# Folding mirrored places before the 49-point products of a Fourier mixer

## Chip, cores and metric

The kernel runs on one core of a Trainium2 chip. The metric is device time in microseconds (us) of one execution. Before the change, three runs took 1089.32, 1090.04 and 1090.96 us, a median of 1090.04 us.

## What is computed

Three layers follow each other on tensors of 2 batches x 3136 tokens x 256 features: a gated attention, a mixer with low rank along the tokens and a two-layer perceptron, and a Fourier mixer with the same kind of perceptron behind it. The change touches the Fourier mixer alone. Cut to what matters:

```python
scores = matmul(z, z.T) / S
x = u * matmul(maximum(scores, 0) ** 2, v)        # attention
u1 = x + ((x.T @ U) @ V).T
x = u1 + maximum(u1 @ w_ch1, 0) @ w_ch2           # first perceptron
X = fft(fft(x, axis=1), axis=2)                   # 3136 tokens, 256 features
u2 = x + real(X)
un = (u2 - mean(u2)) / sqrt(var(u2) + 1e-6)
return u2 + maximum(un @ w2_ch1, 0) @ w2_ch2      # second perceptron
```

## The kernel before

The 3136 tokens are ordered as 64 x 49, so the transform along the tokens is one of length 49 and then one of length 64, and the one along the features is made last. The program has an attention part (up to about 503 us) and a perceptron part. The second goes through 28 chunks of 448 tokens (layer, batch, seventh), and each chunk through 8 steps. One step is written to TensorE in a fixed order: six products of `hidden` (L431 to L433) and six of `project` (L456 to L458) for the hidden part of two steps ago, each 128x128 by 448 columns in float32r with the operands split into a high and a low half. Behind these twelve come the step's guests: the events of the 49-point transform, and one piece of each active generator (`prep1` with the product L321, `fourier` with the products L1179 and L1197 to L1202, `prep2` for the norms). Every engine works its own instructions in the order written; nothing is reordered by a scheduler there. The tables at the end of the program (`starts`, `events`, `folds`, `behind`) set the step of each guest.

The 49-point transform of a batch is made in 8 blocks of 4 token columns (`halves49`). For each block four events follow one another:

- `fold(i)` adds mirrored features on VectorE into `y`, turns them, and writes them to DRAM (`nat_d`).
- `fetch(i)` loads them back with places on partitions (98 rows by 4x128 columns).
- `tokens(i)` makes the high half on ScalarE and the low half on VectorE, and an alternating sum on VectorE.
- `axis49(i)` calls `dft49`: three float32r products of 512 columns (L1140 to L1142) into one PSUM tile, one copy on ScalarE (L133, tile `wst`), and the write to DRAM (`scr`).

Four rows of the 98 belong to each pair of mirrored places, and place 0 has two.

`fourier(b)` starts with `column128`, which treats feature 128 apart: a row is loaded into `raw128`, transposed on TensorE (L1151), split, and multiplied by the same 49-point matrix with 64 columns. Then come the 64-point products (`axis64`, L1179, plain float32, fetched from `scr`) and the feature products (`features`).

All these products take their PSUM tile from `misc()`, which hands out the banks m, x and g in turn. A product that gets a bank waits until the readers of its last content are done:

```python
def misc():
    p, tag = misc_pools[misc_at[0] % len(misc_pools)]
    misc_at[0] += 1
    return p.tile([128, 512], F32, tag=tag, name="ps_" + tag)
```

A plain float32 product stands in the trace as two MATMUL records, each with its own weight load.

Of the kernel before, what the change touches and what calls it, by code (L numbers as in the profile page):

```python
# [24 lines left out]
KPOS = 25  # L25
# [61 lines left out]
def _constants():  # L87

    o1, o2, c1, c2, tok, feat = _orders()
    b49 = np.zeros((98, 128))  # L90
    t2 = 2 * np.pi * ((c2 * np.outer(o2, np.arange(KPOS))) % 49) / 49
    for par in range(2):
        b49[par::2, par * 32 : par * 32 + KPOS] = np.cos(t2)
        b49[par::2, 64 + par * 32 + 1 : 64 + par * 32 + KPOS] = np.sin(t2[:, 1:])
# [28 lines left out]
def program(ctx, tc, zT, v, uT, U, V, w1a, w2a, w1b, w2b, b49, f64, fd, rep, mask, out):  # L123
# [52 lines left out]
    b49h = const.tile([128, 128], F32R, name="b49h")  # L176
    b49l = const.tile([128, 128], F32R, name="b49l")
# [848 lines left out]
    raw128 = mp.tile([128, 112], F32, tag="raw128", name="raw128", bufs=1)  # L1026
# [5 lines left out]
    top = [mp.tile([98, 32], F32, tag=f"top{b}", name=f"top{b}", bufs=1) for b in range(NB)]  # L1032
# [8 lines left out]
    nats = [[mp.tile([128, 512], F32R, tag=f"{t}{k}", name=f"{t}{k}", bufs=1) for t in ("nh", "nl")] for k in range(3)]  # L1041

    def pair_late():
# [6 lines left out]
    def mixer():  # L1050
# [18 lines left out]
        for x in (*nats[0], *nats[1], *nats[2]):  # L1069
            nc.gpsimd.memset(f(x)[96:128], 0.0)  # L1070
# [8 lines left out]
    def halves49(b):  # L1079
# [3 lines left out]
        yv = y[:, 0:392].rearrange("p (s m r) -> p s m r", m=49, r=2)  # L1083

        def fold(i):

            s0, s1 = 4 * i, 4 * i + 4
            for t0, t1 in ((0, 1), (1, s1)) if s0 == 0 else ((s0, s1),):
                for m, w in ((0, 0), (1, 25), (25, 1)):
                    n = 24 if m else 1  # L1090
                    in1 = x1[:, t0:t1, w : w + n]
                    if t0:
                        in1 = in1[:, :, :, ::-1]
                    tt(
                        out=yv[:, t0 - s0 : t1 - s0, m : m + n],
# [3 lines left out]
                    )  # L1099
            yt = mp.tile([128, 416], F32, tag="A1" if i == 7 else "yt", name="yt", bufs=1)  # L1100
# [6 lines left out]
            if i == 7:  # L1107
                load(out=raw128[0:32, 0:98], in_=xT[b][0:1, 1, :].rearrange("o (s p) -> o s p", p=98))

        def alternating(i, x):  # L1110

            v = x[0:98].rearrange("p (s d r) -> p s d r", s=4, r=2)
            t = spare[0:98, 0:256].rearrange("p (s d) -> p s d", s=4)
            sub(t, v[:, :, :, 0], v[:, :, :, 1])
            nc.vector.reduce_sum(out=top[b][0:98, 4 * i : 4 * i + 4], in_=t, axis=mybir.AxisListType.X)

        def fetch(i):
            h, l = nat[i] = pair_late()
            load(
                out=f(l)[0:98].rearrange("p (s d) -> p s d", s=4),  # L1120
                in_=nat_d[b][i, 0:392].rearrange("(s p) d -> p s d", p=98),
            )

        def tokens(i):
            h, l = nat[i]
            hcopy(h[0:98], f(l)[0:98])
            alternating(i, f(l))
            sub(l[0:98], f(l)[0:98], f(h[0:98]))

        def axis49(i):  # L1130
            ps = misc()
            dft49(ps, *nat.pop(i))
            w = mp.tile([128, 512], F32, tag="wst", name="wst")
            hcopy(w, ps)
# [4 lines left out]
    def dft49(ps, h, l):  # L1139
        mm(ps, b49h, h, start=True, stop=False)  # L1140
        mm(ps, b49h, l, start=False, stop=False)
        mm(ps, b49l, h, start=False, stop=True)  # L1142

    def fourier(b):
# [3 lines left out]
        def column128():  # L1148

            ps = misc()  # L1150
            nc.tensor.transpose(ps[0:98, 0:128], raw128[:, 0:98], ident)  # L1151
            h, l = (t[:, 0:64] for t in pair_late())
            for s, x in ((slice(0, 32), ps[0:98, 0:32]), (slice(32, 64), top[b][0:98])):
                hcopy(h[0:98, s], x)
                sub(l[0:98, s], x, f(h[0:98, s]))
            yield
            yield
            ps = misc()
# [260 lines left out]
```

## Time and profile before

| | before |
|---|---|
| median of three runs | 1090.04 us |
| profiled execution, its own time | 1089.02 us |
| span of the profile | 1087.2 us |
| PE busy | 1077.7 us (99%) |
| DVE busy | 848.1 us (78%) |
| ACT busy | 623.2 us (57%) |
| POOL busy | 255.2 us (23%) |
| granted TensorE clock | 1.0 |

The span runs from the first to the last instruction; 1.8 us of the execution's own time lie around it. PE is TensorE's products, PEld its weight loads, DVE is VectorE, ACT ScalarE, POOL GpSimd, SP SyncE. A MATMUL's recorded length is its passage through the array and not the time it takes from its successors; what it costs is the distance from its start to the start of the next.

### The profile page before, as it was taken

Reading aid. Unit: us, or ns where it says so; the run is one execution under the profiler, and the core shown is the slowest. Engines: PE = TensorE matmul, PEld = TensorE weight load, DVE = VectorE, ACT = ScalarE, POOL = GpSimd, SP = SyncE. Lnnn points to the kernel's source line nnn. Section 1 sums busy time; section 2 is a strip of 40 time slices with the busy share of each in tenths; the row PEclk is TensorE's granted clock in tenths of the full one; section 3 lists DMA queues with packets and bytes.
Section 4 is the critical chain, followed back from the end, with each engine's and each line's share of the span. In section 5 each row is a group of like instructions: output and inputs, shape, how many; then the busy total and the mean of one; then the engine's idle time right before and its main releaser. Section 6 shows DMA issues by size and latency. Waiting matters only on the chain.

```text
span 1087.2 us, 21197 instructions
## 1 busy us (share of the span) xinstructions
PE 1077.7 (99%) x7926; PEld 1000.6 (92%) x7926; DVE 848.1 (78%) x1571; ACT 623.2 (57%) x1094; POOL 255.2 (23%) x426
## 2 busy tenths in 40 slices
PE   9999999999999999999999999999999999999998
PEld 7999999999989999989899999999999999999997
DVE  7898888988999987666666776677688888778863
ACT  7888777768897876553434444433355454444431
POOL 2143345222333344221110121121231111011100
PEclk9999999999999999999999999999999999999999
DMA  6356667675667677875523453231253221121210
GB/s 177 94 135 167 179 184 218 210 268 143 167 189 209 177 216 241 268 244 154 183 68 90 143 177 100 78 78 34 64 128 105 62 89 47 35 65 47 60 43 35
DMA packets 140519, 146.04 MB, mean 134 GB/s; under 512 B 72534, under 2 KB 113530, under 8 KB 140416
## 3 DMA queue, kind: packets, MB, share of 16 engines
q1 hardware_dynamic: 108704, 70.57, 22.9%
q0 software_dynamic: 23280, 47.72, 15.5%
q10 hardware_dynamic: 8432, 26.40, 7.7%
q8 instruction: 62, 1.02, 0.4%
q14 instruction: 41, 0.34, 0.1%
HBM read 88.61 MB, written 56.00 MB: 133 GB/s over the span
## 4 chain that ended last, share of the span: by engine, by line
PE 84%; DMA 5%; DVE 4%; ACT 3%; issue 2%; POOL 0%; SPq 0%; ACTq 0%; DVEq 0%; POOLq 0%
PE psO L776 27%; PE psH L431 8%; PE psH L433 8%; PE psC L458 8%; PE psC L456 8%; PE psH L432 8%; PE psC L457 8%; PE psS L722 5%; DMA kept<-turned 1%; DVE l L136 1%; DVE turned L688 1%; DMA uT<-in_uT 1%; ACT P L742 1%; ACT P L743 1%; DMA turned<-kept 1%
## 5 line engine op out<-in xcount | busy, mean ns | idle before, releaser
L776 PE MATMUL psO<-h,Vt 64*128 64x448 f32 x2744 | 323.2, 361 | 2.0 <-DVE h L749 1.0
L776 PEld LDWEIGHTS psO<-h,Vt 64*128 64x128 f32 x2744 | 266.1, 184 | 21.5 <-DVE h L749 3.9
L436 ACT ACTIVATE Hh<-psH 128x448 fp32r<-128x448 f32 x224 | 121.5, 543 | 244.5 <-PE psH L433 241.2
L437 DVE SCALAR_TENSOR_TENSOR Hl<-psH,Hh 128x448 fp32r<-128x448 f32 x224 | 138.0, 618 | 109.8 <-ACT Hh L436 108.0
L136 DVE TENSOR_TENSOR l<-P,h 128x896 fp32r<-128x896 f32 (+2 forms) x188 | 170.6, 914 | 50.6 <-ACT h L133 43.7
L776 PE MATMUL psO<-l,Vt 64*128 64x448 f32 x1372 | 184.7, 360 | 1.4 <-DVE l L136 1.0
L431 PE MATMUL psH<-h,w 128*128 128x448 f32 x448 | 164.9, 368 | 0.0
L433 PE MATMUL psH<-h,w 128*128 128x448 f32 x448 | 162.4, 363 | 0.0
L458 PE MATMUL psC<-Hh,w 128*128 128x448 f32 x448 | 162.4, 362 | 0.0
L432 PE MATMUL psH<-l,w 128*128 128x448 f32 x448 | 162.2, 362 | 0.0
L457 PE MATMUL psC<-Hl,w 128*128 128x448 f32 x448 | 162.1, 362 | 0.0
L456 PE MATMUL psC<-Hh,w 128*128 128x448 f32 x448 | 162.0, 362 | 0.0
L698 POOL DMA_DIRECT2D kept<-turned x178 | 112.3, 636 | 158.2 <-DVE turned L688 124.0
L776 PEld LDWEIGHTS psO<-l,Vt 64*128 64x128 f32 x1372 | 137.9, 184 | 12.1 <-DVE l L136 4.7
L742 ACT ACTIVATE P<-psS 128x896 f32<-128x896 f32 (+1 forms) x124 | 108.0, 871 | 22.6 <-PE psS L722 21.7
L743 ACT ACTIVATE P<-P 128x896 f32<-128x896 f32 (+1 forms) x124 | 113.1, 912 | 3.9
L133 ACT CAST h<-P 128x448 fp32r<-128x448 f32 (+1 forms) x111 | 80.1, 733 | 58.1 <-DVE P L322 39.6
L431 PEld LDWEIGHTS psH<-h,w 128*128 128x128 f32 x448 | 84.1, 188 | 6.2 <-issue 0.3
L457 PEld LDWEIGHTS psC<-Hl,w 128*128 128x128 f32 x448 | 84.0, 187 | 6.1
L432 PEld LDWEIGHTS psH<-l,w 128*128 128x128 f32 x448 | 84.2, 188 | 5.8
L456 PEld LDWEIGHTS psC<-Hh,w 128*128 128x128 f32 x448 | 83.9, 187 | 5.6 <-issue 0.2
L458 PEld LDWEIGHTS psC<-Hh,w 128*128 128x128 f32 x448 | 84.1, 188 | 5.5
(299 smaller groups left out, 1356.6 us busy)
## 6 DMA issues: line engine op xcount, KB each, us to landing
turned<-kept ACTq DMA_DIRECT2D x49, 448.0 KB, 5.5
kept<-turned POOLq DMA_DIRECT2D x102, 112.0 KB, 3.2
uT<-in_uT SPq DMA_DIRECT2D x14, 448.0 KB, 5.0
out<-P SPq DMA_DIRECT2D x27, 224.0 KB, 1.9
aTd<-turned POOLq DMA_DIRECT2D x13, 448.0 KB, 5.9
kept<-turned SPq DMA_DIRECT2D x51, 112.0 KB, 2.0
aNd<-turned POOLq DMA_DIRECT2D x40, 112.0 KB, 3.8
scr<-wst SPq DMA_DIRECT2D x16, 256.0 KB, 2.0
```

The source lines that it names most:

```text
L136: tt(out=o, in0=a, in1=b, op=ALU.subtract)
L431: mm(ps[:, 0:CH], wh, self.h[:, a], start=a == 0, stop=False)
L432: mm(ps[:, 0:CH], wh, self.l[:, a], start=False, stop=False)
L433: mm(ps[:, 0:CH], wl, self.h[:, a], start=False, stop=a == 1)
L436: act(out=h, in_=ps[:, 0:CH], func=AF.Relu)
L437: stt(out=l, in0=ps[:, 0:CH], scalar=0.0, in1=f(h), op0=ALU.max, op1=ALU.subtract)
L456: mm(dst, wh, h, start=k == 0, stop=False)
L457: mm(dst, wh, l, start=False, stop=False)
L458: mm(dst, wl, h, start=False, stop=k == 7)
L742: act(out=A[:, x].rearrange("p (a n) -> p a n", a=2), in_=ps[:, :, 0:w], func=AF.Relu, scale=1.0 / S)
L743: act(out=A[:, x], in_=A[:, x], func=AF.Square)
L776: mm(o[fa][i][:, 0:CH], vt[r, j, k, fa * 128 : fa * 128 + 128], x[r, j * CH : j * CH + CH], start=n0 == 0 and fa not in [t[1][0] for t in ...
```

## The change

In `fold`, the sums of mirrored features first go to a spare tile `ya`; two further VectorE instructions then write the sums and the differences of mirrored places into `y`. The rows come back as 50 sums on partitions 0 to 49 and 48 differences on partitions 64 to 111, with two loads in place of one. The split into a high and a low half goes. `dft49` becomes four products of 64x64 by 256 columns in plain float32: rows 0 to 63 and rows 64 to 127, each with a column half of its own, into two banks. Three ScalarE copies take the result out in place of one. `column128` folds its row on VectorE before the transpose.

```diff
-        late_dma(out=t[0:98, 0:128], in_=b49)
+        late_dma(out=b49s, in_=b49)
...
-        for x in (b49h, b49l):
-            nc.gpsimd.memset(f(x), 0.0)
-        hcopy(b49h[0:98], t[0:98, 0:128])
-        sub(b49l[0:98], t[0:98, 0:128], f(b49h[0:98]))
...
+    ya, row128 = spare[:, 256:640], spare[0:32, 640:752]
...
                     tt(
-                        out=yv[:, t0 - s0 : t1 - s0, m : m + n],
+                        out=yw[:, t0 - s0 : t1 - s0, m // 25] if m else yv[:, t0 - s0 : t1 - s0, 0:1],
...
+            for m, op in ((1, ALU.add), (25, ALU.subtract)):
+                tt(out=yv[:, :, m : m + 24], in0=yw[:, :, 0], in1=yw[:, :, 1], op=op)
...
         def fetch(i):
-            h, l = nat[i] = pair_late()
-            load(
-                out=f(l)[0:98].rearrange("p (s d) -> p s d", s=4),
-                in_=nat_d[b][i, 0:392].rearrange("(s p) d -> p s d", p=98),
-            )
+            t = nat[i] = nat_late()
+            src = nat_d[b][i, 0:392].rearrange("(s p) d -> p s d", p=98)
+            for at, p0, n in ((0, 0, 50), (64, 50, 48)):
+                load(out=t[at : at + n].rearrange("p (s d) -> p s d", s=4), in_=src[p0 : p0 + n])
 
         def tokens(i):
-            h, l = nat[i]
-            hcopy(h[0:98], f(l)[0:98])
-            alternating(i, f(l))
-            sub(l[0:98], f(l)[0:98], f(h[0:98]))
+            alternating(i, nat[i])
...
-    def dft49(ps, h, l):
-        mm(ps, b49h, h, start=True, stop=False)
-        mm(ps, b49h, l, start=False, stop=False)
-        mm(ps, b49l, h, start=False, stop=True)
+    def dft49(out, x):
+
+        ps, n = (misc(), misc()), out.shape[1] // 2
+        even, odd = slice(0, 64), slice(64, 128)
+        for j in range(2):
+            for r, to in ((even, (even, odd)[j]), (odd, (odd, even)[j])):
+                mm(ps[j][to, 0:n], b49s[r, r], x[r, j * n : j * n + n], start=True, stop=True)
+        hcopy(out[:, 0:n], ps[0][:, 0:n])
+        hcopy(out[even, n : 2 * n], ps[1][odd, 0:n])
+        hcopy(out[odd, n : 2 * n], ps[1][even, 0:n])
...
         def column128():
 
+            pair = [row128[:, c : c + 48] for c in (2, 50)]
+            nc.vector.tensor_copy(raw128[0:32, 0:2], row128[:, 0:2])
+            tt(out=raw128[0:32, 2:50], in0=pair[0], in1=pair[1], op=ALU.add)
+            sub(raw128[0:32, 64:112], *pair)
             ps = misc()
-            nc.tensor.transpose(ps[0:98, 0:128], raw128[:, 0:98], ident)
-            h, l = (t[:, 0:64] for t in pair_late())
-            for s, x in ((slice(0, 32), ps[0:98, 0:32]), (slice(32, 64), top[b][0:98])):
-                hcopy(h[0:98, s], x)
-                sub(l[0:98, s], x, f(h[0:98, s]))
+            nc.tensor.transpose(ps[:, 0:128], raw128, ident)
+            t = nat_late()[:, 0:64]
+            hcopy(t[:, 0:32], ps[:, 0:32])
+            hcopy(t[:, 32:64], top[b])
             yield
             yield
-            ps = misc()
-            dft49(ps[:, 0:64], h, l)
             w = mp.tile([128, 512], F32, tag="wst", name="wst")[:, 0:64]
-            hcopy(w, ps[:, 0:64])
+            dft49(w, t)
```

The lines that the diff doesn't touch stand five earlier in the changed kernel up to the mixer (L431 becomes L426), and the products of `dft49` are L1139 there.

The order moves in three places that matter. The first is VectorE in the step in which `column128` of batch 0 begins; `raw` is the row of feature 128 that TensorE transposes at the end of that step, L466 (now L461) the last additions of a chunk of the first perceptron. Before:

```order
L437 SCALAR_TENSOR_TENSOR Hl<-psH,Hh 128x448 x3
L466 TENSOR_TENSOR xT_7721<-psC_9230,P 128x448
L466 TENSOR_TENSOR xT_7721<-psC_9231,P 128x448
L136 TENSOR_TENSOR nl_7737<-ps_x,nh_7736 98x32
L136 TENSOR_TENSOR nl_7737<-top_7728,nh_7736 98x32
```

And now:

```order
L432 SCALAR_TENSOR_TENSOR Hl<-psH,Hh 128x448 x3
L461 TENSOR_TENSOR xT_7716<-psC_9252,P 128x448
L461 TENSOR_TENSOR xT_7716<-psC_9253,P 128x448
L1151 COPY raw_7717<-Us 32x2
L1152 TENSOR_TENSOR raw_7717<-Us 32x48
L136 TENSOR_TENSOR raw_7717<-Us 32x48
L432 SCALAR_TENSOR_TENSOR Hl<-psH,Hh 128x448 x2
```

Where VectorE read the transposed row (`ps_x`) after TensorE, it now makes the row (`raw`) before TensorE, behind the same two additions.

The second is VectorE at the same point of batch 1, where a norm (L402 to L353, now L397 to L348) stands ahead. Now:

```order
L432 SCALAR_TENSOR_TENSOR Hl<-psH,Hh 128x448 x2
L397 RECIPROCAL vr<-vy 32x14
L398 TENSOR_TENSOR vy<-vr 32x14
L399 TENSOR_TENSOR vy<-vy,ve 32x14
L400 TENSOR_SCALAR vy<-vy 32x14
L401 TENSOR_TENSOR pad<-vy,vr 32x14
L348 STREAM_TRANSPOSE vt<-pad 32x32
L1151 COPY raw_7717<-Us 32x2
L1152 TENSOR_TENSOR raw_7717<-Us 32x48
L136 TENSOR_TENSOR raw_7717<-Us 32x48
```

The three instructions that make the row stand behind the whole norm, where before two that read the transposed row stood.

The third is TensorE at the one block (batch 1, block 1) that comes behind the generators of its step (table `behind`). Before:

```order
L321 MATMUL ps_x<-Vs,Gs_100 128x448
L1197 MATMUL ps_g<-Th,fA 128x384
L1198 MATMUL ps_g<-Tl,fA 128x384
L1199 MATMUL ps_g<-Th,fA 128x384
L1200 MATMUL ps_m<-Th,fB 128x384
L1201 MATMUL ps_m<-Tl,fB 128x384
L1202 MATMUL ps_m<-Th,fB 128x384
L1140 MATMUL ps_x<-nh_7734,b49h 128x512
L1141 MATMUL ps_x<-nl_7735,b49h 128x512
L1142 MATMUL ps_x<-nh_7734,b49l 128x512
```

And now, from the first feature product on:

```order
L1198 MATMUL ps_m<-Th,fA 128x384
L1199 MATMUL ps_m<-Tl,fA 128x384
L1200 MATMUL ps_m<-Th,fA 128x384
L1201 MATMUL ps_x<-Th,fB 128x384
L1202 MATMUL ps_x<-Tl,fB 128x384
L1203 MATMUL ps_x<-Th,fB 128x384
L1139 MATMUL ps_g<-nt_7728,b49s 64x256 x2
L1139 MATMUL ps_m<-nt_7728,b49s 64x256 x2
```

The block took the bank that `prep1` had used (x); now it takes two, the one that `prep1` used (g) and the one that the feature products of the same step wrote just before (m).

## Rows read from the trace of the kernel before

**Rows 1.** The page, part 1: busy time, share and instructions of TensorE.
```profile
PE 1077.7 (99%) x7926; PEld 1000.6 (92%) x7926; DVE 848.1 (78%) x1571; ACT 623.2 (57%) x1094; POOL 255.2 (23%) x426
```
**Rows 2.** Waits of TensorE from 505 us on: total us, times, longest.
```profile
PE ps_m L1179 <- DMA wr<-scr: 0.5, 1, 0.5
```
**Rows 3.** Timeline of TensorE, one block: start us, length us, instruction, form.
```profile
610.78 0.39 PE L1140 MATMUL ps_m<-nh,b49h 128*128 128x512 f32 x1
...
611.47 0.36 PE L431 MATMUL psH<-h,w 128*128 128x448 f32 x1
```
**Rows 4.** Timeline of TensorE, plain float32 products in four column tiles.
```profile
535.48 0.36 PE L321 MATMUL ps_x<-Vs,Gs 128*128 128x448 f32 x1
535.76 2.80 PE L282 MATMUL ps_g<-xT,Us 128*32 128x256 f32 x48
538.38 0.29 PE L286 MATMUL ps_g<-row,Us 128*32 128x64 f32 x8
...
538.91 0.36 PE L432 MATMUL psH<-l,w 128*128 128x448 f32 x1
```
**Rows 5.** Timeline of TensorE, the 49-point products of feature 128, batch 0.
```profile
676.93 0.19 PE L1140 MATMUL ps_g<-nh,b49h 128*128 128x64 f32 x1
...
677.47 0.36 PE L432 MATMUL psH<-l,w 128*128 128x448 f32 x1
```
**Rows 6.** Timeline of TensorE, transpose of the row of batch 0.
```profile
672.02 0.27 PE L1151 MATMUL ps_x<-ident,raw 128*98 128x128 f32 x1
```
**Rows 7.** Timeline of VectorE, the same step.
```profile
672.13 1.14 DVE L466 TENSOR_TENSOR xT<-psC,P 128x448 f32<-128x448 f32 x2
673.19 0.18 DVE L136 TENSOR_TENSOR nl<-ps_x,nh 98x32 fp32r<-98x32 f32 x1
673.29 0.18 DVE L136 TENSOR_TENSOR nl<-top,nh 98x32 fp32r<-98x32 f32 x1
```
**Rows 8.** Timeline of TensorE, transpose of the row of batch 1.
```profile
827.14 0.27 PE L1151 MATMUL ps_x<-ident,raw 128*98 128x128 f32 x1
```
**Rows 9.** Timeline of VectorE, the same step.
```profile
828.35 0.20 DVE L353 STREAM_TRANSPOSE vt<-pad 32x32 f32<-32x32 f32 x1
828.49 0.14 DVE L136 TENSOR_TENSOR nl<-ps_x,nh 98x32 fp32r<-98x32 f32 x1
```
**Rows 10.** Timeline of TensorE, first 64-point product of batch 1, with its wait.
```profile
835.43 0.68 PE L1179 MATMUL ps_m<-f64s,wr 128*128 128x128 f32 x4 [0.47 <-DMA wr<-scr]
```
**Rows 11.** Timeline of TensorE, the block behind the generators.
```profile
727.25 0.39 PE L1140 MATMUL ps_x<-nh,b49h 128*128 128x512 f32 x1
```
**Rows 12.** Timeline of VectorE, the same step: readers of the banks.
```profile
726.41 0.62 DVE L322 TENSOR_TENSOR P<-ps_x,xT 128x448 f32<-128x448 f32 x1 [0.20 <-PE ps_x L321]
...
728.21 0.61 DVE L1205 SCALAR_TENSOR_TENSOR A<-row,maskc,ps_g 128x384 f32<-128x384 f32 x1
```
**Rows 13.** Timeline of TensorE, batch 1, block 0: its last product.
```profile
703.30 0.39 PE L1142 MATMUL ps_x<-nh,b49l 128*128 128x512 f32 x1
```
**Rows 14.** Timeline of ScalarE, the copy of that block.
```profile
703.73 0.59 ACT L133 COPY wst<-ps_x 128x512 f32<-128x512 f32 x1 [1.34 <-PE ps_x L1142]
```
**Rows 15.** Groups of VectorE, 537 to 835 us, by form: busy us, mean ns.
```profile
L136 DVE TENSOR_TENSOR nl<-nl,nh 98x512 fp32r<-98x512 f32 x16 | 10.9, 684 | 1.4 <-ACT nh L133 1.4
...
L1094 DVE TENSOR_TENSOR y<-xT 128x192 f32<-128x192 f32 x28 | 8.7, 351 | 0.0
```
**Rows 16.** Groups of ScalarE, 537 to 905 us, by form.
```profile
L133 ACT CAST nh<-nl 98x512 fp32r<-98x512 f32 x16 | 9.9, 616 | 1.7 <-DMA nl<-natd 1.5
L133 ACT COPY wst<-ps_m 128x512 f32<-128x512 f32 x8 | 4.7, 588 | 9.0 <-PE ps_m L1142 8.9
L133 ACT CAST Th<-ps_m 128x256 fp32r<-128x256 f32 x9 | 3.3, 367 | 4.9 <-PE ps_m L1179 4.9
```
**Rows 17.** Timeline of VectorE behind the fold of batch 0, block 1.
```profile
566.28 1.12 DVE L437 SCALAR_TENSOR_TENSOR Hl<-psH,Hh 128x448 fp32r<-128x448 f32 x2
```
**Rows 18.** Timeline of TensorE, first product of `project` that needs it.
```profile
567.15 0.36 PE L456 MATMUL psC<-Hh,w 128*128 128x448 f32 x1
```

More of the change, by code (lines that the diff above doesn't have):

```diff
@@ L89, in _constants @@
     o1, o2, c1, c2, tok, feat = _orders()
-    b49 = np.zeros((98, 128))
+    b49 = np.zeros((128, 128))
     t2 = 2 * np.pi * ((c2 * np.outer(o2, np.arange(KPOS))) % 49) / 49
     for par in range(2):
-        b49[par::2, par * 32 : par * 32 + KPOS] = np.cos(t2)
-        b49[par::2, 64 + par * 32 + 1 : 64 + par * 32 + KPOS] = np.sin(t2[:, 1:])
+        b49[par : 50 : 2, par * 32 : par * 32 + KPOS] = np.cos(t2[:KPOS])
+        b49[64 + par : 112 : 2, 64 + par * 32 + 1 : 64 + par * 32 + KPOS] = np.sin(t2[1:KPOS, 1:])
     t1 = 2 * np.pi * ((c1 * np.outer(o1, o1)) % 64) / 64
@@ L175, in program @@
     maskc = const.tile([128, 16], F32, name="maskc")
-    b49h = const.tile([128, 128], F32R, name="b49h")
-    b49l = const.tile([128, 128], F32R, name="b49l")
+    b49s = const.tile([128, 128], F32, name="b49s")
     f64s = const.tile([128, 128], F32, name="f64s")
@@ L1023, in program @@
     xT = late["xT"] = [xpool.tile([128, 2, S], F32, tag=f"xT{b}", name=f"xT{b}") for b in range(NB)]
-    raw128 = mp.tile([128, 112], F32, tag="raw128", name="raw128", bufs=1)
+    raw128 = mp.tile([128, 176], F32, tag="raw128", name="raw128", bufs=1)[:, 0:128]
     col128 = mp.tile([128, 128], F32, tag="col128", name="col128", bufs=1)
@@ L1031, in program @@
     spare = Us.rearrange("p a n -> p (a n)")
-    top = [mp.tile([98, 32], F32, tag=f"top{b}", name=f"top{b}", bufs=1) for b in range(NB)]
+    ya, row128 = spare[:, 256:640], spare[0:32, 640:752]
+    top = [mp.tile([128, 32], F32, tag=f"top{b}", name=f"top{b}", bufs=1) for b in range(NB)]
     for t in (raw128, col128, y[:, 392:416]):
@@ L1039, in program, with nat_late @@
     late["small"] = small
-    nats = [[mp.tile([128, 512], F32R, tag=f"{t}{k}", name=f"{t}{k}", bufs=1) for t in ("nh", "nl")] for k in range(3)]
-    def pair_late():
+    nats = [mp.tile([128, 512], F32, tag=f"nt{k}", name=f"nt{k}", bufs=1) for k in range(3)]
+    def nat_late():
         nats.append(nats.pop(0))
@@ L1067, in mixer @@
         yield
-        for x in (*nats[0], *nats[1], *nats[2]):
-            nc.gpsimd.memset(f(x)[96:128], 0.0)
+        for x in nats:
+            for r in (quads[1], quads[3]):
+                nc.gpsimd.memset(x[r], 0.0)
         P = small()[:, 0:D]
@@ L1083, in halves49 @@
         yv = y[:, 0:392].rearrange("p (s m r) -> p s m r", m=49, r=2)
+        yw = ya.rearrange("p (s h m r) -> p s h m r", h=2, m=24, r=2)
         def fold(i):
@@ L1107, in fold @@
             if i == 7:
-                load(out=raw128[0:32, 0:98], in_=xT[b][0:1, 1, :].rearrange("o (s p) -> o s p", p=98))
+                load(out=row128[:, 0:98], in_=xT[b][0:1, 1, :].rearrange("o (s p) -> o s p", p=98))
         def alternating(i, x):
-            v = x[0:98].rearrange("p (s d r) -> p s d r", s=4, r=2)
-            t = spare[0:98, 0:256].rearrange("p (s d) -> p s d", s=4)
+            v = x.rearrange("p (s d r) -> p s d r", s=4, r=2)
+            t = spare[:, 0:256].rearrange("p (s d) -> p s d", s=4)
@@ L1114, in alternating @@
             sub(t, v[:, :, :, 0], v[:, :, :, 1])
-            nc.vector.reduce_sum(out=top[b][0:98, 4 * i : 4 * i + 4], in_=t, axis=mybir.AxisListType.X)
+            nc.vector.reduce_sum(out=top[b][:, 4 * i : 4 * i + 4], in_=t, axis=mybir.AxisListType.X)
         def fetch(i):
-            h, l = nat[i] = pair_late()
-            load(
-                out=f(l)[0:98].rearrange("p (s d) -> p s d", s=4),
-                in_=nat_d[b][i, 0:392].rearrange("(s p) d -> p s d", p=98),
-            )
+            t = nat[i] = nat_late()
@@ L1133, in axis49 @@
             w = mp.tile([128, 512], F32, tag="wst", name="wst")
[L1134 removed]
+            dft49(w, nat.pop(i))
             load(out=scr[b][:, 4 * i : 4 * i + 4, :], in_=w.rearrange("p (s d) -> p s d", s=4))
         return fold, fetch, tokens, axis49
[L1139 to L1142 removed]
+    def dft49(out, x):
[7 more added lines that the diff above has]
+        hcopy(out[odd, n : 2 * n], ps[1][even, 0:n])
```

2 lines of the change are left out of this document (removed).

## Prediction

> **What bounds the kernel now.** I read the busy shares first: TensorE is busy 99% of the span [rows 1]. Then its waits from 505 us on, where all that the change touches lies: one wait of 0.5 us in all [rows 2]. So the perceptron part is a full queue of products. VectorE and ScalarE have room there, and what they save is worth nothing by itself; a microsecond counts if TensorE streams longer or shorter, switches, or begins to wait. Then the timeline of TensorE around one block, the start-to-start distances being the price [rows 3], the only place where plain float32 products run in tiles of the array [rows 4], and the timelines of VectorE and ScalarE where the order moves [rows 6 to 9, 11 to 14].
>
> **Blocks: streaming.** A block now costs TensorE 611.47 - 610.78 = 0.69 us for three products of 512 columns [rows 3], so a product of 448 columns, the common size, costs 0.20. The new block has four plain float32 products of 256 columns, each two passes. A round of passes over 256 columns in four column tiles at once takes (538.38 - 535.76)/12 = 0.218 us: the 48 records are 12 rounds of 4 [rows 4]. If the four 64x64 tiles run together as those four do, a block streams 2 x 0.218 = 0.44 us.
>
> **Blocks: the switch.** Rows 4 show also what leaving the full array costs. The product ahead (535.48) would be followed after 0.20 us, at 535.68; behind, L432 at 538.91 means that full products go on as if from 538.71. In these 3.03 us stand twelve rounds (2.62) and two of 64 columns (a quarter of 0.218 each, 0.11); 0.30 us are left for the way in and out. A 64-column weight load is seen nowhere and lies between that of 32 columns there and the 128 of the way out, so I take 0.34; bounds 0.25 and 0.45. A block is then 0.44 + 0.34 = 0.78 us, 0.09 more than now; 16 blocks: **+1.4 us** (bounds 0 to +3.2).
>
> No row shows two row halves of the array writing one bank at a time; the nearest is rows 4, where four column tiles write one bank at once, in different partitions, and lose nothing. Here the first two products share a bank in just that way, in different partitions, so I take all four together. A rule speaks against it: the Trainium skill, "TensorEngine Tiling (Array Packing)", section Restrictions and Gotchas, says that different row tiles cannot access the same PSUM bank at the same time. By that rule a block would need four rounds and not two, and the sum would be the first rival's; rows 4 have only one row tile and cannot refute it.
>
> **Feature 128.** Its three products of 64 columns cost 677.27 - 676.93 = 0.34 us per batch, where 677.27 is L432 less 0.20 [rows 5]. The new ones have 32 columns: two rounds at 0.055 and a switch, 0.45. Two batches: **+0.2 us**.
>
> **Feature 128: the new wait.** Before, the transpose needed only a row that had long been loaded. Now it needs three VectorE instructions, which stand where the readers of its result stood. In batch 0, TensorE comes to the transpose at 672.02 [rows 6]; VectorE is in the two additions that close a chunk until 673.19 [rows 7], and these need products that ended just before. Three small operations at the 0.10 us from one to the next and the 0.17 of the last [rows 7] end at 673.56; TensorE goes on about 0.04 later (as a copy follows a product by 0.04 in rows 13 and 14). That is 673.6 - 672.02 = **+1.6 us** (bounds 1.4 and 1.9). In batch 1, it comes there at 827.14 [rows 8], and VectorE reaches the place at 828.49, behind a norm that begins with the hidden part of the same step [rows 9]. 828.49 + 0.37 + 0.04 = 828.90: **+1.75 us** (bounds 1.6 and 2.0). All products of the following steps are queued behind both transposes. One thing is given back: the 0.47 us that TensorE waits for a transfer at 835.43 [rows 10] set by a chain through the last block's copy and not by TensorE; arriving 1.75 us later, it finds the data there even if the three copies lengthen that chain by 0.3. **-0.5 us**.
>
> **Two banks in place of one.** With three banks in turn, I followed each block to the last user of its banks. Two places meet a reader that is late. In batch 1, block 1, the second bank is the one that the feature products wrote just before. Its reader runs from 728.21 to 728.82 [rows 12], and TensorE is at the block at 727.25 [rows 11]. The first two products run; the other two start at 728.86, and with 0.44 of streaming and 0.20 for the way out the next full product starts at 729.50, not at 727.25 + 0.78 = 728.03: **+1.5 us** (bounds 1.2 and 1.7). The first bank is free in time, as its reader ends at 727.03 [rows 12]. In batch 1, block 0, a 64-point product of the same step gets the bank of the first copy. A copy follows the last product by 703.73 - 703.30 = 0.43 us [rows 13, 14], and 256 columns take 0.37 [rows 16]; TensorE has one product of 0.20 to do meanwhile: **+0.2 us** (0 to 0.5). Everywhere else at least one step (twelve products of 0.20, 2.4 us) lies between.
>
> **VectorE and ScalarE.** Per block VectorE loses a subtraction of 684 ns and gains two additions of the size that takes 351 [rows 15]; ScalarE loses a cast of 616 and makes three copies of about 0.3 each for one of 588 [rows 16]. Even, and covered by TensorE's queue. The gain and the loss fall in different steps, though: the fold grows by 0.6 us. Its tightest follower is batch 0, block 1: the first of two low halves behind the fold ends at 566.86, half of the 1.12 [rows 17], and the product that needs it starts at 567.35, the second of `project` [rows 18]. Margin 0.5, so **+0.1 us**. The second load per block is one more issue on SyncE, and it delays VectorE's alternating sum by as much, with microseconds in hand before the product. The constants go one cast and one subtraction lighter in the attention part: nothing. If one of these covers failed, its price would be the 0.3 to 0.6 us of that instruction, each time.
>
> **Sum.** +1.4 + 0.2 + 1.6 + 1.75 - 0.5 + 1.5 + 0.2 + 0.1 = +6.2 us. The profiled execution took 1089.02 us (span 1087.2 and 1.8 around it), so the sum gives 1095.2; it lay 1.0 under the median of 1090.04, which gives **1096.2 us**. A measurement of this kernel can tell 0.2%, or 2.2 us, from no change.
>
> **Rivals.** *Two by two.* Products that share a bank from different row halves take turns. Each block streams 0.88 us; the block of batch 1 that waits anyway loses nothing more, so 15 x 0.44 = +6.6 on top: 1102.8. For it: no row shows the contrary. Against it: the four tiles of rows 4 share a bank freely. The rule named above would do just this. *One by one* (+0.44 x 3 x 16 = 21, 1117) has only a remote chance, as rows 4 show tiles at work together.
>
> *No price for the switch* (the other side). If weights for 64x64 tiles are loaded behind the running full-array product, 18 times 0.34 us fall away, -6.1, and the streaming gain of 0.25 per block pays for all waits: 1090.1, no slower than now. It decides at a switch of about 0.1 us, where the change falls to under 0.2%. Against it: the 0.30 of rows 4.
>
> *Waits that don't come.* If VectorE finds the three row operations early enough, or the bank is free, 3 to 4 us go and some 1092 is left. Against it: both depend on products that end only then, whatever VectorE saves.
>
> **From these to the numbers.** Forecast 0.74, its own range 1093 to 1099.5, from the bounds of the switch (-1.4 to +1.8), the transposes (-0.4 to +0.6) and the banks (-0.5 to +0.5), not all at one end. Two by two 0.13, one by one 0.02, no price for the switch 0.06, no waits 0.05. To leave out no more than 2 in 10, the range goes down to the case without waits and up to two by two: 1092 to 1103. Faster by over 0.2% (under 1087.9) needs a free switch and short waits: 0.03. Within 0.2%: the rest of that case, most of the one without waits: 0.08. Slower: 0.89.
>
> **What would show it.** Right: four MATMUL records of L1139 starting within some 30 ns, twice per block; 0.75 to 0.85 us from a block's first record to where L426 would stand; waits of TensorE on VectorE at both transposes and in one block on bank m; no wait at the first 64-point product of batch 1. Wrong: pairs of records 0.2 us apart within a bank (two by two), a block of 0.5 us (free switch), or no idle TensorE at the transposes. A granted clock under 1.0 or a wait of `project` on VectorE elsewhere would mean that I missed a cover.

## The result and the profile after

The changed kernel takes 1097.18 us (median of six runs, 1096.20 to 1098.31), the kernel before 1089.81 (six runs, 1089.25 to 1090.96): a ratio of 1.0067, 95% interval 1.0054 to 1.0080. It is slower by 7.4 us, inside the range and 1.0 us over the forecast. The profiled execution took 1096.88 us with a span of 1095.1, at a granted clock of 1.0.

The page of after, part 1, against [rows 1]: TensorE is as full as before, with 3.9 us more of busy time.

```profile
PE 1081.6 (99%) x8016; PEld 995.5 (91%) x8016; DVE 848.4 (77%) x1588; ACT 623.4 (57%) x1113; POOL 255.0 (23%) x424
```

The waits of TensorE in after, of which two are new from 505 us on and the one of [rows 2] is gone (total us, times, longest):

```profile
PE ps_m L1155 <- DVE raw L136: 3.2, 2, 1.7
...
PE ps_m L1139 <- DVE A L1206: 0.9, 1, 0.9
```

One block on TensorE in after (start us, length us, instruction, form), against [rows 3]:

```profile
611.72 0.37 PE L453 MATMUL psC<-Hh,w 128*128 128x448 f32 x1
612.01 0.43 PE L1139 MATMUL ps_x<-nt,b49s 64*64 64x256 f32 x2
612.03 0.43 PE L1139 MATMUL ps_g<-nt,b49s 64*64 64x256 f32 x2
612.28 0.38 PE L1139 MATMUL ps_x<-nt,b49s 64*64 64x256 f32 x2
612.29 0.38 PE L1139 MATMUL ps_g<-nt,b49s 64*64 64x256 f32 x2
612.61 0.47 PE L426 MATMUL psH<-h,w 128*128 128x448 f32 x1
612.92 0.36 PE L427 MATMUL psH<-l,w 128*128 128x448 f32 x1
```

Each line holds two records, the two row halves of one bank, and all four start within 20 ns, twice. The next full product would have started at 611.92; L427 at 612.92 means that full products go on as if from 612.72. A block is 0.80 us.

The transpose of the row of batch 0 on TensorE in after, against [rows 6]:

```profile
675.63 0.30 PE L1155 MATMUL ps_m<-ident,raw 128*128 128x128 f32 x1 [1.54 <-DVE raw L136]
```

VectorE of after in that step, against [rows 7]: the three instructions of the row stand behind the two additions. The last ends at 675.48, and TensorE starts 0.15 us later.

```profile
674.05 1.15 DVE L461 TENSOR_TENSOR xT<-psC,P 128x448 f32<-128x448 f32 x2
675.11 0.15 DVE L1151 COPY raw<-Us 32x2 f32<-32x2 f32 x1
675.18 0.19 DVE L1152 TENSOR_TENSOR raw<-Us 32x48 f32<-32x48 f32 x1
675.29 0.19 DVE L136 TENSOR_TENSOR raw<-Us 32x48 f32<-32x48 f32 x1
```

The block behind the generators on TensorE in after, against [rows 11] (x4 holds both rounds of one bank):

```profile
731.56 0.65 PE L1139 MATMUL ps_g<-nt,b49s 64*64 64x256 f32 x4
733.09 0.65 PE L1139 MATMUL ps_m<-nt,b49s 64*64 64x256 f32 x4 [0.88 <-DVE A L1206]
733.67 0.47 PE L426 MATMUL psH<-h,w 128*128 128x448 f32 x1
733.98 0.36 PE L427 MATMUL psH<-l,w 128*128 128x448 f32 x1
```

VectorE of after, the reader of bank m, against [rows 12]: it runs to 733.03, and the second bank's products start 0.06 us later.

```profile
732.42 0.61 DVE L1206 SCALAR_TENSOR_TENSOR A<-row,maskc,ps_m 128x384 f32<-128x384 f32 x1
```

To place every microsecond I took the first low-half product of `hidden` (L432, now L427) of each of the 224 steps, and its start in one trace less its start in the other. Where this difference jumps, a step grew or shrank. Before against after:

| place | forecast, us | measured, us |
|---|---|---|
| 16 blocks | +1.4 | +1.5 (0.09 to 0.12 at 13 that stand alone; 0.10 counted here at the two that also wait; none at the block of [rows 3]) |
| products of feature 128 | +0.2 | +0.23 |
| transpose of batch 0 | +1.6 | +1.73 |
| transpose of batch 1 | +1.75 | +1.88 |
| wait for `wr` | -0.5 | -0.71 |
| bank wait, batch 1, block 1 | +1.5 | +1.51 |
| bank wait, batch 1, block 0 | +0.2 | +0.36 |
| fold of batch 0, block 1 | +0.1 | +0.34 |
| two small places | 0 | +0.16 |
| attention part | 0 | +0.75 |
| sum | +6.2 | +7.9 |

The sum is that of the two profiled executions (1096.88 - 1089.02); the rows leave out differences of under 0.05 us in a step. The block of [rows 3] grew by 0.11 us like the others, from 0.69 to 0.80, but its step lost as much, since a pause of TensorE ahead of it in the trace of before is not there in after.

### The profile page after: what moved, and what is told of

The parts are those of the page before. It is cut to its first block, busy times and chain, and to the rows that moved or that the text cites. A ratio compares the mean times of both kernels' runs of the same rounds, so it can differ in the third digit from the quotient of the medians.

```text
span 1095.1 us, 21440 instructions
## 1 busy us (share of the span) xinstructions
PE 1081.6 (99%) x8016; PEld 995.5 (91%) x8016; DVE 848.4 (77%) x1588; ACT 623.4 (57%) x1113; POOL 255.0 (23%) x424
## 4 chain that ended last, share of the span: by engine, by line
PE 85%; DVE 6%; ACT 3%; DMA 3%; issue 2%; POOL 0%; ACTq 0%; DVEq 0%; POOLq 0%
PE psO L771 28%; PE psH L426 8%; PE psC L453 8%; PE psH L428 8%; PE psC L452 8%; PE psH L427 8%; PE psC L451 8%; PE psS L717 4%; DVE l L136 2%; DVE turned L683 1%; DMA uT<-in_uT 1%; ACT P L737 1%; ACT P L738 1%; DMA kept<-turned 1%; ACT h L133 1%
## 5 line engine op out<-in xcount | busy, mean ns | idle before, releaser
L771 PE MATMUL psO<-h,Vt 64*128 64x448 f32 x2744 | 321.7, 361 | 2.8 <-DVE h L744 1.6
L771 PEld LDWEIGHTS psO<-h,Vt 64*128 64x128 f32 x2744 | 265.7, 184 | 21.8 <-DVE h L744 5.2
L431 ACT ACTIVATE Hh<-psH 128x448 fp32r<-128x448 f32 x224 | 121.2, 542 | 245.7 <-PE psH L428 240.6
L432 DVE SCALAR_TENSOR_TENSOR Hl<-psH,Hh 128x448 fp32r<-128x448 f32 x224 | 137.9, 617 | 112.0 <-ACT Hh L431 109.9
L771 PE MATMUL psO<-l,Vt 64*128 64x448 f32 x1372 | 183.0, 360 | 1.3 <-DVE l L136 1.0
L426 PE MATMUL psH<-h,w 128*128 128x448 f32 x448 | 166.0, 371 | 0.0
L452 PE MATMUL psC<-Hl,w 128*128 128x448 f32 x448 | 162.4, 363 | 0.1
L453 PE MATMUL psC<-Hh,w 128*128 128x448 f32 x448 | 162.5, 363 | 0.0
L427 PE MATMUL psH<-l,w 128*128 128x448 f32 x448 | 162.4, 362 | 0.0
L771 PEld LDWEIGHTS psO<-l,Vt 64*128 64x128 f32 x1372 | 136.8, 184 | 11.4 <-DVE l L136 4.4
L426 PEld LDWEIGHTS psH<-h,w 128*128 128x128 f32 x448 | 84.2, 188 | 9.1 <-issue 3.8
L452 PEld LDWEIGHTS psC<-Hl,w 128*128 128x128 f32 x448 | 84.0, 188 | 6.7 <-DVE Hl L432 0.8
L451 PEld LDWEIGHTS psC<-Hh,w 128*128 128x128 f32 x448 | 83.9, 187 | 6.0 <-ACT vv L133 0.4
L427 PEld LDWEIGHTS psH<-l,w 128*128 128x128 f32 x448 | 84.2, 188 | 5.4
L428 PEld LDWEIGHTS psH<-h,w 128*128 128x128 f32 x448 | 84.0, 188 | 5.4
```

The lines of the kernel that those rows point to most:

```text
L426: mm(ps[:, 0:CH], wh, self.h[:, a], start=a == 0, stop=False)
L427: mm(ps[:, 0:CH], wh, self.l[:, a], start=False, stop=False)
L428: mm(ps[:, 0:CH], wl, self.h[:, a], start=False, stop=a == 1)
L431: act(out=h, in_=ps[:, 0:CH], func=AF.Relu)
L432: stt(out=l, in0=ps[:, 0:CH], scalar=0.0, in1=f(h), op0=ALU.max, op1=ALU.subtract)
L451: mm(dst, wh, h, start=k == 0, stop=False)
```

## Experiments

Ratios are to the kernel before, run on the same chip beside each; gains and losses by place are read from the traces as in the table above.

**The kernel before once more**, with no edit.

> The kernel before, unchanged, once more: a second trace of it. The changed kernel's trace lies 0.75 us behind already where the attention part ends (first product of hidden at 503.83 + 0.75), where the change moves almost nothing. Theory: that part drifts by some tenths of a us from run to run, so this trace differs from the first one there by 0.3 to 1 us, while the steps of the perceptron part lie within 0.05 us each. Rival: the change sets it (other addresses, other constants): then this trace meets the first one within 0.1 us at the end of the attention part.

One execution took 1090.32 us. Its attention part ended 0.72 us later than in the first trace of the same kernel. All steps of the perceptron part agree within 0.05 us but the one of [rows 10], which is 0.61 longer, since the wait there was 1.08 us and not 0.47. So the theory held but for this one step: the +0.75 of the attention part needs no cause in the change, and the wait for `wr` is worth 0.5 to 1.1 us.

**The row early.** The three instructions that make the row of feature 128 move from `column128` to the last block's `tokens`:

```diff
         def tokens(i):
             alternating(i, nat[i])
+            if i == 7:
+                pair = [row128[:, c : c + 48] for c in (2, 50)]
+                nc.vector.tensor_copy(raw128[0:32, 0:2], row128[:, 0:2])
+                tt(out=raw128[0:32, 2:50], in0=pair[0], in1=pair[1], op=ALU.add)
+                sub(raw128[0:32, 64:112], *pair)
...
         def column128():
-            pair = [row128[:, c : c + 48] for c in (2, 50)]
...
```

> The changed kernel, with the three VectorE instructions that make the row of feature 128 moved three steps earlier, into the event tokens of block 7. Theory (TensorE waits in order for VectorE): the waits of 1.7 and 1.8 us at the two transposes go, and the wait of 0.5 to 0.7 us at the first 64-point product of batch 1 comes back: 2.6 to 3.0 us less than the changed kernel, about 1094.4. Rival (the time is only moved): VectorE is behind in those steps too, project waits for it in place of the transpose, and less than 1 us is won.

1094.54 us (1094.07 to 1095.48), ratio 1.0044 (1.0029 to 1.0058): 2.6 us less than the changed kernel, as expected. Both waits at the transposes are gone, and the steps shrink by 1.72 and 1.87 us, all that they had grown by. But the wait for `wr` did not return; 0.89 us came back elsewhere, at a product of `project` in the second perceptron. Of TensorE's waits in this run from 505 us on:

```profile
...
PE psC L452 <- DVE Hl L432: 0.6, 1, 0.6
```

VectorE was late there because it had waited for the mean of a norm:

```profile
DVE P L376 <- DMA mu<-mud: 4.8, 2, 2.7
```

Five more of the traces below lost 0.2 to 0.9 us at this step, the others nothing. VectorE's longest wait for this transfer is 0.3 and 0.5 us in the two traces of the kernel before and 0.8 to 2.7 in all ten of the changed kernels, so the change may have a part in it; its cause was not tried.

**The block first.** The block of batch 1, block 1 goes ahead of the generators of its step:

```diff
-                    table = folds if op is ops[0] else behind if op is ops[3] and (b, k) == (1, 1) else events
+                    table = folds if op is ops[0] else events
```

> The changed kernel, with the one block that stood behind the generators of its step (batch 1, block 1) put ahead of them as the others are. Theory (the wait is for the bank that the feature products just wrote): the 1.1 us gap inside that block and the switch-out paid late go, 1.2 to 1.5 us less than the changed kernel; at most 0.3 us of it returns as waits of the feature products on the block's copies. Rival (the wait moves): the feature products wait for the three copies as long as the block did for VectorE, and nothing is won.

1096.70 us (1095.35 to 1098.36), ratio 1.0067 (1.0051 to 1.0084). The step shrank by 0.92 us, less than the 1.2 to 1.5 expected, and 0.69 us of its growth stays, 0.1 of it the block itself. The wait has turned round: now the feature products want the banks of the block. TensorE in this run:

```profile
730.12 0.47 PE L316 MATMUL ps_x<-Vs,Gs 128*128 128x448 f32 x1
730.67 0.44 PE L1198 MATMUL ps_g<-Th,fA 128*128 128x384 f32 x1
```

And ScalarE, whose copy of bank g ends at 730.62:

```profile
730.25 0.37 ACT L133 COPY wst<-ps_g 128x256 f32<-128x256 f32 x1 [1.27 <-PE ps_m L1139]
```

L1198 starts 0.55 us behind L316, where 0.20 is usual. The median does not resolve the gain.

**The products twice.** The loop over the four products runs two times, into the same banks.

```diff
+        for _ in range(2):
             for j in range(2):
```

> The changed kernel with the four products of every block, and of feature 128, issued twice in a row into the same banks, so that each excursion into 64x64 tiles streams 4 rounds of 256 columns and not 2, with one way in and one way out as before. Theory (a block is 0.44 us of streaming at 0.218 us a round, all four tiles together, and a fixed 0.35 us for the switch): each of the 16 blocks grows by 0.44 us, each product of feature 128 by 0.11, so the whole by 7.0 + 0.2 = 7.2 us, less about 0.4 at the block of batch 1 that waits anyway: 1104.0, ratio to the changed kernel about 1.0062. Rival (the tiles do not really overlap, and the starts 20 ns apart hide queueing, so the block's 0.80 us is all streaming): each block grows by about 0.8 us, the whole by some 12 to 13 us, 1109.5. Rival (the price is a cost per record, of 16 weight loads of 64 columns a block): also about 0.8 us a block.

1103.80 us (1102.89 to 1104.19), ratio 1.0132 (1.0118 to 1.0146): 6.6 us over the changed kernel. Each of the 16 blocks grew by 0.41 to 0.44 us, feature 128 by 0.13 and 0.12. One block of this run on TensorE:

```profile
612.19 0.43 PE L1140 MATMUL ps_x<-nt,b49s 64*64 64x256 f32 x2
...
612.45 0.38 PE L1140 MATMUL ps_x<-nt,b49s 64*64 64x256 f32 x2
...
612.67 0.38 PE L1140 MATMUL ps_x<-nt,b49s 64*64 64x256 f32 x2
...
612.88 0.38 PE L1140 MATMUL ps_x<-nt,b49s 64*64 64x256 f32 x2
...
613.21 0.47 PE L426 MATMUL psH<-h,w 128*128 128x448 f32 x1
```

Four rounds some 0.22 us apart. Two more rounds cost 0.435, so a round is 0.218, and of the block's 0.80 us 0.80 - 0.435 = 0.365 is the switch. All four tiles run together: both rivals asked for about 0.8 a block.

**The full array.** `dft49` becomes one plain float32 product of 128x128 by 512 columns into one bank, with one copy; the folded rows and the rest stay.

```diff
-        ps, n = (misc(), misc()), out.shape[1] // 2
...
+        ps, n = misc(), out.shape[1]
+        mm(ps[:, 0:n], b49s, x, start=True, stop=True)
+        hcopy(out, ps[:, 0:n])
```

> The changed kernel, with the four 64x64 products of a block made one 128x128 product of 512 columns (the matrix has zeros outside its two diagonal blocks), plain float32, one bank, one copy. Twice the columns stream, no tile mode is entered. Theory (a fixed 0.35 us per switch, 0.43 per two rounds of 256 columns): a block costs 0.86 to 0.88 us in place of 0.80, 16 x 0.07 = +1.1; feature 128 costs 0.22 in place of 0.45, -0.5; one bank in place of two, so the waits at blocks 0 and 1 of batch 1 go, -1.9. In all -1.3 us, about 1095.9, with the transposes' waits unchanged. Rival (streaming is the price, the switch costs little): 0.86 against about 0.45 per block, +6.5 us, 1102 or more less the bank waits.

1096.41 us (1095.04 to 1096.77), ratio 1.0057 (1.0042 to 1.0072). On TensorE in this run:

```profile
613.46 1.02 PE L1136 MATMUL ps_m<-nt,b49s 128*128 128x512 f32 x2
613.91 0.76 PE L426 MATMUL psH<-h,w 128*128 128x448 f32 x1
614.52 0.36 PE L427 MATMUL psH<-l,w 128*128 128x448 f32 x1
```

A block is 614.52 - 0.20 - 613.46 = 0.86 us: twice the streaming of the tiles and no switch. The four tiles save 0.43 us of streaming and pay 0.365 of it for the way in and out. Both bank waits vanish (-1.45 and -0.29 against after), as one bank is taken and not two; the products of feature 128 lose 0.23 each; the transposes wait nearly as in after. All steps together are 1.6 us shorter than in after, where 1.3 were expected; the medians show half of it, 0.8. The rival, a switch that costs little (1102 or more), fell.

**Pairs.** Blocks 2k and 2k+1 share one excursion, in the two column halves of the same two banks; only the last two of batch 1 stay single.

```diff
+            if not (b and i > 5):
+                if i % 2 == 0:
+                    return
+                ws = [mp.tile([128, 512], F32, tag="wst", name="wst") for _ in range(2)]
+                dft49s(ws, [nat.pop(i - 1), nat.pop(i)])
```

> The changed kernel with two blocks in one excursion: the products of blocks 2k and 2k+1 are issued together, into the two column halves of the same two banks, in the step of the second; only the last two blocks of batch 1 stay single, as the data of both come in time only so. 7 ways in and out fewer. Theory (the switch is a fixed 0.35 us for each excursion): a pair takes 0.88 + 0.35 = 1.23 us where two single blocks take 1.60, so 7 x 0.35 = 2.5 us go, 1094.7; ratio to the changed kernel about 0.9977. In batch 1 the pair of blocks 0 and 1 stands in the step of block 1 and still waits for its bank, now with four copies behind it and three, so that up to 1 us may come back. Rival (the time of a block is streaming or a cost per record): nothing but noise moves, 1097.2 within 0.7.

1098.09 us (1096.24 to 1099.06), ratio 1.0078 (1.0065 to 1.0091): no gain, a miss by 3.4 us. The blocks did what was expected, some 0.37 us less for each pair, 7 times. What follows is the trace of the slowest execution, 1099.06 us. In it the gain went elsewhere. The pair of batch 0 with blocks 6 and 7 has six copies on ScalarE, in the step ahead of the row. They end at 674.28, the hidden part behind them (L431 on ScalarE) begins at 674.31 and not at 672.93 as in after, and VectorE makes the row later by what that delays it. TensorE at the transpose in this run:

```profile
676.92 0.48 PE L1177 MATMUL ps_x<-ident,raw 128*128 128x128 f32 x1 [2.42 <-DVE raw L136]
677.05 0.72 PE L426 MATMUL psH<-h,w 128*128 128x448 f32 x1
677.57 0.57 PE L427 MATMUL psH<-l,w 128*128 128x448 f32 x1
677.95 0.57 PE L428 MATMUL psH<-h,w 128*128 128x448 f32 x1
...
680.43 0.37 PE L451 MATMUL psC<-Hh,w 128*128 128x448 f32 x1
```

Busy time in the stretch behind it (start and end, length, busy us of PE, PEld, DVE, ACT, POOL, then the granted clock, DMA share, GB/s):

```profile
677.00:681.00 4.00, 4.00 (x13) 3.61 (x14) 0.62 (x1) 0.85 (x3) 0.00 (x0) 0.59 0.23 65
```

The wait grew from 1.54 to 2.42 us, and behind it the products are 0.37 us apart and not 0.20: the granted clock is at its lower level, 1.2 GHz, for most of that stretch. Nine products take 3.38 us, 677.05 to 680.43; the same nine take 1.89 in after (675.69 to 677.58). So the longer wait cost 0.9 us and the clock 1.5 on top. The norm's wait took 0.9 more, and the attention part of this execution, which the edit does not touch, was 1.9 us longer; part of that is another stretch at the lower clock, shown in the last section. Not every execution was hit alike: of the five, the one whose mean granted clock was 1.0 took 1096.24 us, the other four, at 0.997 and 0.998, 1097.04 to 1099.06.

**The fold light.** The two additions that make sums and differences of mirrored places are left out for batch 0, block 1 alone; its places in `y` keep what stood there.

```diff
-            for m, op in ((1, ALU.add), (25, ALU.subtract)):
+            for m, op in ((1, ALU.add), (25, ALU.subtract)) if (b, i) != (0, 1) else ():
```

> The changed kernel without the two further additions of one fold, that of batch 0, block 1: the sums and differences of mirrored places of that block are not made, and its places in y keep what stood there. The loads, products and copies of the block are all there. Theory (that fold makes VectorE late for the low half of the hidden part, and the second product of project waits 0.34 us for it): that step gets 0.3 us shorter than in the changed kernel, with no wait of TensorE there, all else alike, 1096.9 (a third of a microsecond is to be seen in the trace of the step, not in the median). Rival (the 0.34 us is the other part of the step, the second load's issue or a run's own scatter): the step stays as long as in the changed kernel.

1097.33 us (1096.88 to 1097.89), ratio 1.0074 (1.0060 to 1.0088). The step is 0.34 us shorter, all of its growth. TensorE in this run, where the second product of `project` waits no more (0.20 us behind the first):

```profile
568.66 0.36 PE L451 MATMUL psC<-Hh,w 128*128 128x448 f32 x1
568.86 0.36 PE L452 MATMUL psC<-Hl,w 128*128 128x448 f32 x1
```

The theory held, though the median cannot show it.

**Three edits together**: pairs, the row early, the pair of batch 1 with blocks 0 and 1 ahead of the generators.

> The changed kernel with three edits together: two blocks in one excursion, the three row operations in the last block's tokens and not ahead of the transpose, and the pair of batch 1 with blocks 0 and 1 ahead of the generators of its step. Theory (each part has a cause and a price of its own): 1097.2 - 2.5 for seven switches - 2.7 for the transposes with what comes back in a norm - 0.9 for the block = 1091.1, from 1090 to 1092, ratio to the kernel before 1.001. The streaming itself gains, as a pair takes 1.23 us where two blocks of the kernel before take 1.38, but only 7 x 0.15 = 1 us, which the late fold and feature 128 use up. Rival (the parts hide each other, as time gained at one place is lost at the next wait): 1093 or more.

1091.94 us (1091.36 to 1092.97), ratio 1.0025 (1.0016 to 1.0034), inside the 1090 to 1092 expected. The prices add up; the clock stays at 1.0. The largest losses left against the kernel before are the fold (0.36), a feature product that waits 1.2 us for a copy of the pair ahead of it, 0.4 us in which `project` waits for VectorE behind the copies of batch 0's last pair, and 0.38 at the norm.

**The row later.** The other way round, to test the clock alone: three more additions on scratch ahead of the row.

```diff
         def column128():
+            for _ in range(3):
+                tt(out=ya[:, 0:192], in0=ya[:, 0:192], in1=ya[:, 0:192], op=ALU.add)
```

> The changed kernel with three additions of 192 columns more on VectorE (scratch, read by nobody) ahead of the three that make the row of feature 128, so that TensorE waits about 0.95 us longer at both transposes, 2.5 and 2.7 us where it was 1.54 and 1.74. Theory (in the run with pairs a wait of 2.4 us at this place was followed by 3.4 us at a granted clock of 0.5, which cost 1.3 us more than the wait itself; the clock falls because TensorE stood still that long): after both transposes some 8 or 9 products are 0.37 us apart and not 0.20, so each place costs 0.95 + 1.3 to 1.7 us, the whole +4.5 to +5.3: 1101.7 to 1102.5. Rival (the low clock in that run came from something else, such as the pairs): the clock stays at 1.0 and the whole grows by the 1.9 us alone, 1099.1.

1101.86 us (1101.53 to 1102.48), ratio 1.0113 (1.0098 to 1.0129): 4.7 us over the changed kernel, as the theory had it, where the added waiting is 2.1 (2.59 and 2.72 us where it was 1.54 and 1.67). TensorE at the second transpose in this run:

```profile
839.52 0.30 PE L1157 MATMUL ps_m<-ident,raw 128*128 128x128 f32 x1 [2.72 <-DVE raw L136]
...
840.67 0.48 PE L428 MATMUL psH<-h,w 128*128 128x448 f32 x1
840.95 0.57 PE L451 MATMUL psC<-Hh,w 128*128 128x448 f32 x1
841.32 0.57 PE L452 MATMUL psC<-Hl,w 128*128 128x448 f32 x1
```

Busy time by stretch, columns as above, around both transposes:

```profile
677.00:681.00 4.00, 4.00 (x13) 3.61 (x14) 0.62 (x1) 0.85 (x3) 0.00 (x0) 0.58 0.26 73
...
838.00:842.00 4.00, 2.48 (x10) 2.30 (x11) 1.48 (x8) 0.85 (x3) 1.07 (x2) 0.85 0.42 100
842.00:846.00 4.00, 4.00 (x16) 3.49 (x15) 1.88 (x4) 0.94 (x3) 0.00 (x0) 0.73 0.33 82
```

The low clock comes without pairs, behind both waits; behind the second it sets in over 1.1 us after the restart at 839.52, as the product of 840.67 is the first whose successor comes late. With the waits gone (the row early) it stays at 1.0. So in this place the low clock follows the long standstill.

**Two copies.** All blocks in pairs; each bank is taken out by one copy, and the exchange of the row halves is left to the write to DRAM; the fold of batch 0, block 1 comes four steps later; the row early and the block first as above.

```diff
+        for out, bank in zip(outs, ps):
+            hcopy(out, bank)
...
+                load(out=to[:, 0], in_=a)
+                for r, q in ((slice(0, 64), slice(64, 128)), (slice(64, 128), slice(0, 64))):
+                    load(out=to[r, 1], in_=z[q])
...
+                at = 26 if (b, k) == (0, 1) else at
```

> All blocks in pairs, the row early and the pair of batch 1 with blocks 0 and 1 ahead of the generators, as in the run with three edits together, and two edits more. Each bank of a pair is taken out by one ScalarE copy of 512 columns (two of 0.59 us, and not six of 0.37), since the exchange of the two row halves is left to the write to DRAM, three transfers for a pair; and the fold of batch 0, block 1 comes four steps later, where VectorE has 1.84 us idle. Theory (of the 2.4 us by which the run with three edits lay above the kernel before, 1.2 are a feature product that waits for the six copies, 0.4 a product that waits for VectorE behind the same copies, 0.35 the fold): 1091.9 - 0.9 - 0.4 - 0.35 - 0.4 for the last two blocks = 1089.9 or below, and by the steps (8 pairs at 1.23 us for two blocks at 0.69, -1.2; feature 128 +0.2; a rest of the bank wait +0.3; the norm's wait between 0 and +0.4; the transfer wait between -0.7 and 0) 0.7 to 1.7 us under the kernel before: about 1088.5, ratio 0.999. Rival (the copies are not what is waited for, or three transfers for a pair make the 64-point products late): 1091 or more.

1089.73 us (1088.31 to 1090.83, eleven runs), ratio 1.0000 (0.9991 to 1.0009). Its waits of TensorE from 505 us on; the second is the one that was 1.2 us in the run with three edits, cut to 0.3:

```profile
PE psC L452 <- DVE Hl L432: 0.6, 1, 0.6
PE ps_x L1215 <- ACT wst L133: 0.3, 1, 0.3
```

All that the change had lost is back, and nothing is won: eight pairs gain some 1.2 us and the shorter wait for `wr` 0.4, and the norm's wait, 0.89 in this trace, feature 128 (0.2) and the rest of the bank wait (0.6) use it up. Of the two values expected, 1089.9 or below came out and 1088.5 did not. No version here beats the kernel before.

## Why the prediction was right, and where it was off

*Streaming and switch.* 0.44 + 0.34 = 0.78 forecast for a block, 0.435 + 0.365 = 0.80 measured. The product rows in four column tiles [rows 4] were a good measure of both.

*Two by two* fell: the two row halves that share a bank start together in every block, and doubled products cost 0.435 and not 0.87. The Trainium skill, "TensorEngine Tiling (Array Packing)", section Restrictions and Gotchas, says that different row tiles cannot access the same PSUM bank at the same time. Here they do, in different partitions of it: the two halves start within 20 ns, and a round of all four tiles takes 0.218 us, as in [rows 4]. Two row halves that write the same partitions of a bank were not tried. *No price for the switch* fell with the same rows, and the pairs showed the switch a second time: 0.37 us less for each excursion saved.

*The transposes.* The mechanism held, with 1.73 and 1.88 us measured for the 1.6 and 1.75 forecast; moving the three instructions took all of it back. The forecast was short by 0.13 each time. It let TensorE go on 0.04 us behind the last operation, read off a copy behind a product [rows 13, 14]; from VectorE to TensorE it was 0.15 and 0.14.

*What is given back.* The wait for `wr` is gone, as forecast, but the reason given was only half of it, and the term came right in part by luck. With the row early, TensorE arrives as soon as before, and the wait is still gone: the first load behind the last block's write to `scr` was issued 2.2 us after that write (831.35 to 833.58) and not 5.1 us, as in the trace of before (825.82 to 830.89). With the full array it took 4.4 us, TensorE was late, and there was no wait either. Both traces of the kernel before have 5.0 and 5.1 us here, the other nine of the changed kernels 2.1 to 3.0, so the change itself seems to shorten it; why a write of 256 KB takes 2 or 5 us stays open.

*The banks.* 1.51 for the forecast 1.5 at the block behind the generators. At batch 1, block 0 the term was 0.2 and measured 0.36, inside its bounds of 0 and 0.5. The one-bank product removed both, so taking two banks was the cause.

*The fold* was the term furthest off by ratio, 0.34 for 0.1. VectorE of after behind this fold, against [rows 17]:

```profile
567.76 1.12 DVE L432 SCALAR_TENSOR_TENSOR Hl<-psH,Hh 128x448 fp32r<-128x448 f32 x2
```

And TensorE, against [rows 18]:

```profile
567.97 0.37 PE L451 MATMUL psC<-Hh,w 128*128 128x448 f32 x1
568.40 0.47 PE L452 MATMUL psC<-Hl,w 128*128 128x448 f32 x1
568.71 0.37 PE L453 MATMUL psC<-Hh,w 128*128 128x448 f32 x1
```

L452 starts 0.08 us behind the half of 1.12, at 568.40 in place of 568.17: 0.23 late. L453 comes 0.31 behind it and not 0.20: 0.11 more. So the forecast put the lateness at 0.1 where it was 0.23, and did not count the 0.11 that TensorE lost in starting again after the pause. That the fold is the cause is shown by the run with the light fold.

*VectorE and ScalarE.* One reading was off: the three copies take 0.37 us each, as [rows 16] have it for 256 columns, and not about 0.3. Nothing hung on it, as 1.1 us is still no more than the cast and the copy of before, 616 and 588 ns.

*The sum* was short by 0.9 in the perceptron part (7.1 for 6.2), made of these small terms, nearly all on one side, and by 0.75 in the attention part, which moves by as much between executions of one kernel. The medians differ by less than the two traces, 7.4 us for 7.9, so that the forecast missed by only 1.0 is in part chance. What the forecast did not see is how near it was to worse: it took a wait to cost its own length, which holds for 1.54 and 1.67 us and no longer for 2.4.

## What to carry to other kernels

A product that streams half as long in tiles of the array wins only what its excursion leaves: here 0.43 us saved against the full array and 0.365 paid, so tiles are worth it when several products share one excursion. Against the three float32r products of before, 0.69 us a block, one block in tiles loses 0.11 and a pair gains 0.15. When a change takes a conversion away, look at what took its place in the order: work put between a transfer and a transpose turned an engine with microseconds in hand into the one that TensorE waits for. And the wait, not the removed work, decides: 3.6 of the 7.1 us lost in the perceptron part came from three instructions of 0.1 us each that stood in the wrong step.

## What the runs showed of the hardware

A wait can cost more than its length. At the same place of the attention part, two executions stood still for nearly the same time ahead of L771. With the full array the wait was 1.71 us and the granted clock stayed at 1.0; with the pairs it was 1.79, and the clock was at 0.52 for the 3.5 us from 417.5 on. These are the rows of the run with pairs, TensorE first and the stretch behind it, columns as under *Pairs*:

```profile
416.63 0.68 PE L771 MATMUL psO<-l,Vt 64*128 64x448 f32 x4 [1.79 <-DVE l L136]
```

```profile
417.50:421.00 3.50, 3.50 (x24) 3.13 (x22) 2.57 (x6) 3.20 (x7) 0.70 (x2) 0.52 0.64 201
```

And of the run with the full array:

```profile
417.08 1.07 PE L771 MATMUL psO<-l,Vt 64*128 64x448 f32 x8 [1.71 <-DVE l L136]
```

```profile
417.00:418.00 1.00, 0.92 (x10) 0.87 (x12) 0.97 (x4) 0.00 (x0) 1.00 (x2) 1.00 0.82 276
...
420.00:421.00 1.00, 1.00 (x11) 0.52 (x7) 0.62 (x1) 1.00 (x4) 0.00 (x0) 1.00 0.23 33
```

The length of this one wait does not tell the two apart, and what does is not shown.

At the transposes, waits of 1.44 to 1.7 us left the clock at 1.0 in all traces, and those of 2.42, 2.59 and 2.72 us were each followed by 1.2 GHz for about 3 us, worth 1.3 to 1.6 us each. The changed kernel's waits there, 1.54 and 1.67 us, were less than a microsecond shorter than the shortest of these.

Plain float32 tiles: four 64x64 tiles with 256 columns take 0.218 us a round, the same as four 128x32 tiles [rows 4], and the way in and out is 0.365 us for one block and for two.
